# Maxima of attention one to two units ahead of the weights, and the selecting matrix loaded at the head of the second half

## The chip, the cores and the metric

The kernel runs on one core of a Trainium2 chip. The metric is device time in microseconds: the median over runs of one launch, lower is better. The engines are PE (matrix products), DVE (elementwise and reductions), ACT (activations), POOL (elementwise, selects, and issuing of some DMAs) and SP (issuing of DMAs). Each has its own instruction order and waits for the others by semaphores. A wait blocks everything that stands behind it on the same engine.

## The reference

The output is `g * a + (1 - g) * b` for 2048 positions of 448 channels, with a gate `g` of each position. `a` is a state space model applied as a long convolution, `b` is an attention in four segments with a memory that is carried from segment to segment:

```python
x = A_u                                              # 1 x 2048 x 448
g = sigmoid((x * gate_w).sum(-1, keepdims=True))
# a: kernel of 2048 taps for each channel, from 256 complex modes
P = exp((A * dt[:, None])[:, :, None] * pos)
K = 2.0 * einsum("dn,dnl->dl", C, P).real
a = irfft(rfft(u_t, 2 * L) * rfft(K, 2 * L))[:, :, :L]  (+ u * D_skip)
# b: 16 heads of 28, four segments s of 512 positions
logits = einsum("bhqd,bhkd->bhqk", qs, ks) * scale + mask      # causal in the segment
a_dot = einsum("bhqk,bhkd->bhqd", softmax(logits), vs)
a_mem = einsum("bhld,bhde->bhle", phi(qs), M) / (phi(qs) . z + 1e-6)
o = sigmoid(beta) * a_mem + (1 - sigmoid(beta)) * a_dot
M, z = M + phi(ks)^T vs, z + sum(phi(ks))
b = o @ wo
```

## The kernel before, in words

**First half** (to about 455 us): the modes' powers and the kernel K, and the projections to q, k and v, which are written to memory in a high and a low part each. Its order is written out, and the change leaves it alone.

**Second half** (`second_half`, L1256). It begins with `attend` (constants and the functions of attention), the loads of unit 0, `transform_k` (K's first step, eight steps long, 456 to 488 us) and `convolve` (the generator `cv`: spectra of the input, products with K's, and back). Then comes a loop over 16 **units** i of attention, each one segment and four heads (a "head group"), and in each unit six **rounds** r. Everything is written as generators; `step(x)` runs one of them up to its next yield. The order in which steps are called is PE's order; the other engines' orders follow nearly the same, with a scheduler free to move what isn't pinned.

What a unit consists of:

- `maxima(i)`, L1028: six steps. Each multiplies the high part of q with that of k for one block of the 512 x 512 logits and one pair of heads (PE, `ps_a<-ku,qu`), and DVE takes the maximum of each row (L1048, with the mask `mk` added). A seventh step does nothing. The eighth turns the maxima over (four transposes on PE, L1433, to `ps_m`), negates and splits them in a high part (ACT, L1058) and a low part (DVE, L1059), and POOL issues two DMAs (`qu<-mn`, L1061) that write them to row 28 of each head in the two parts of q.
- `weigh(i)`, L1064: six steps. Since k has ones in row 28, the products of q and k (PE, `ps_a<-qu,ku`, three products of parts for each tile, six matmuls or twelve) come out with the maximum subtracted. ACT takes exp (`PT`, L1081). After the sixth, POOL zeroes the upper triangles (L1086). The first matmul of each step reads row 28 of the high part, the fifth that of the low part.
- `values(i)`, L1088: at the second step, round 1 of the following unit, PT times V (`ps_pv<-PT,V`) and a copy.
- For segments, `seg_end`: normalising, recalling the memory and the product with `wo`; for the last segment `divide` and `last_end`.

Beside the units run, in the same loop: `rest` (projections of the input's spectra, units 1 to 8, rounds 1, 3, 4, 5; its results are multiplied with the spectra in `pr`, L611), `cv` (1.15 steps in each round of units 1 to 12), the last rows of the convolution in units 14 and 15, and `turn_over(n)`: n **dummy** matmuls of a constant (`ps_pv<-wz`), whose results nobody reads.

`ps_a` has three buffers, shared by maxima, weights and `rest`; `ps_m` and `ps_pv` have one each. So a step of PE waits until the step three before it has been read, by DVE (maxima) or ACT (exp).

Where the maxima stand: unit 0's are stepped among K's first step; two steps of unit 1's too, and four more between that and the loop, with three dummies each:

```python
for r in range(4):
    turn_over(3)
    step(ms[1])
```

In the loop, each round of unit i steps the maxima of unit i + 2 (`ahead`), and the seventh and eighth step of unit i + 1's (`behind`) come in rounds 0 and 1. `load(i + 3)` and `load_rest(i + 2)` at the head of each unit fetch q and k on SP's queue.

`load_wo`, L984, called at the end of unit 1, fills constants: `wo`, `den`, the row `dbc`, and `sel`, the **selecting matrix**. For that one, SP loads `selin` (L992) and ACT copies it to `sel` with rounding (L993). It is used first when the first segment is recalled.

Of the kernel before, what the change touches and what calls it, by code (L numbers as in the profile page):

```python
# [12 lines left out]
F32 = mybir.dt.float32  # L13
# [14 lines left out]
SEG = 512  # L28
# [948 lines left out]
def attend(nc, k, ap):  # L977
# [2 lines left out]
    wo = ap.tile([128, 4, D], F32, name="wo")  # L980
    k.den = ap.tile([128, 128], F32, name="den")
    k.sel = ap.tile([32, 4, 128], F32R, name="sel")

    def load_wo():  # L984
        nc.gpsimd.memset(wo, 0.0)
        for j in range(4):
            k.ldma(
                wo[32 * j : 32 * j + 28], k.wo.rearrange("(g j e) c -> j e g c", j=4, e=28)[j]
            )
        k.ldma(k.den, k.c_den)  # L990
        t = ap.tile([128, 4, SEG], F32, tag="am", name="selin", bufs=1)[:32, 0]
        k.ldma(t, k.c_sel.rearrange("p g c -> p (g c)"))  # L992
        nc.scalar.activation(k.sel.rearrange("p g c -> p (g c)"), t, AF.Copy)  # L993
        k.ldma(k.dbc, k.D_skip.unsqueeze(0).broadcast_to([128, D]))

    Q, K, W, Vs, pvss = {}, {}, {}, {}, {}
# [130 lines left out]
    am = {}  # L1127
# [128 lines left out]
def second_half(nc, k, ap, tp, fp, fin, lp):  # L1256

    none = object()  # L1260

    def step(g):
        return next(g, none) is not none

    nothing = iter(())
    attend(nc, k, ap)
    k.load(0)
    k.load_rest(0)


    wz = ap.tile([128, SEG], BF16, name="wz")
    nc.gpsimd.memset(wz, 1.0)

    def turn_over(n):
        pt = k.ps("pv")
        for _ in range(n):
            k.mm(pt, wz[:, :128], wz, start=True, stop=True)

    first = transform_k(nc, k, tp)
    ms = {i: k.maxima(i) for i in range(16)}  # L1280
    for r in range(8):
        step(first)
        if r == 1:
            k.load(1)
            k.load_rest(1)
        for _ in range((0, 1, 2, 1, 2, 1, 1, 0)[r]):
            step(ms[0])
        if r >= 6:
            step(ms[1])

    pm = k.ps("m")
    k.tr(pm[:16, :128], k.gt, k.ident)
    g16 = ap.tile([16, 128], F32, name="g16")
    nc.vector.tensor_copy(g16, pm[:16, :128])
    k.dma(k.GD.rearrange("(i p) -> i p", p=128), g16)
    k.gt2 = ap.tile([128, 16], F32, name="gt2")
    for h in range(2):
        k.dma(k.gt2[64 * h : 64 * h + 64], k.GD.rearrange("(n h w) -> h n w", h=2, w=16)[h])
    fp = fp()
    cv = convolve(nc, k, fp)  # L1300
    step(cv)
    k.load(2)
    vals = k.values(0)
    step(vals)
    for r in range(4):
        turn_over(3)
        step(ms[1])
    rest = project_rest(nc, k, lp())
    ends = []
    acc = 0.0  # L1310
    n = 0
    for i in range(16):
        k.load_rest(i + 2)
        k.load(i + 3)
        ahead = ms.get(i + 2, nothing)
        behind = ms.get(i + 1, nothing)
        w = k.weigh(i)
        for r in range(6):
            if 1 <= i < 9:
                if r in (1, 3, 4, 5):  # L1320
                    step(rest)
            elif r in WARM:
                turn_over(WARM[r])
            if i == 9 and r == 1:
                step(rest)
            step(ahead)
            step(w)
            if r == 0:
                step(behind)
            if r == 1:  # L1330
                if i > 0:
                    step(vals)
                step(behind)
                if i % 4 == 0 and i > 0:
                    ends.append(k.seg_end(i // 4 - 1))
            if r != 1 or i == 13:
                for _ in range(2 if i == 13 else 1):
                    while ends and not step(ends[0]):
                        ends.pop(0)
            if (i, r) in DIVIDE:  # L1340
                k.divide(DIVIDE[i, r])
            if 1 <= i <= 12:
                acc += RATIO
                while acc >= 1.0:
                    acc -= 1.0
                    step(cv)
            if i == 11 and r == 2:
                k.skip_last()
            if i == 13 and r < 5:
                load_b(r)  # L1350
            if i == 14 and r >= 2 or i == 15 and r < 4:
                last(n)
                turn_over(1)
                if n < 2:
                    join(n + 6)
                if n < 3:
                    load_b(n + 5)
                n += 1
        step(w)
        if i == 1:  # L1360
            k.load_wo()
        if i > 0:
            vals = k.values(i)
            step(vals)
        if i == 12:
            for _ in cv:
                pass
            load_b, join, last = finish(nc, k, fin())
        if i == 13:
            for wc in range(6):  # L1370
                join(wc)
    for e in ends:
        for _ in e:
            pass
    k.last_end(step, vals)
# [1 line left out]

RATIO = 1.15
WARM = {3: 1, 4: 3, 5: 3}
DIVIDE = {(14, 2): 0, (14, 5): 1, (15, 3): 2}  # L1380

# [286 lines left out]
```

## Time and profile before

| | us |
|---|---|
| median of 3 runs | 900.52 |
| lowest and highest | 894.51, 901.75 |
| the profiled execution | 905.99 |
| its span | 904.2 |
| PE busy | 767.8 (85%) |
| DVE busy | 600.0 (66%) |
| ACT busy | 537.1 (59%) |
| POOL busy | 191.0 (21%) |

The profile comes from one execution, which took 905.99 us; the span is from its first to its last recorded instruction. Rows of a timeline begin with the start in the span and the busy time of the group, then engine, line, operation, result and operands, and the number of instructions; in brackets the idle time ahead of it and what ended it. PEclk is the share of TensorE's full clock that was granted, in 40 slices of the span in tenths (9 is 90% and more), or in a window as a fraction. "DMA to landing" is the time from the issue of a DMA to its last byte.

### The profile page before, as it was taken

To read this page: it belongs to the slowest core of one execution; us is meant where nothing else is said; L and a number is where in the kernel's file an instruction comes from. 1 tells how busy PE (TensorE), PEld (TensorE's weight loads), DVE (VectorE), ACT (ScalarE), POOL (GpSimd) and SP (SyncE) were. 2 spreads that over 40 slices of the span, in tenths; PEclk is the share of its full clock that TensorE was granted. 3 is DMA by queue.
4 is the path that set the end of the run, shared out by engine and by line. 5 is a ranking of instruction groups with operands and counts; after the bars stand their busy time and mean duration, and the time that the engine had idled before them with its cause. 6 is when DMAs were issued, how large, how long until landed. Compare 5 with 4: busy or idle time off the path is not lost.

```text
span 904.2 us, 19002 instructions
## 1 busy us (share of the span) xinstructions
PE 767.8 (85%) x7508; PEld 413.7 (46%) x7517; DVE 600.0 (66%) x1158; ACT 537.1 (59%) x640; POOL 191.0 (21%) x273
## 2 busy tenths in 40 slices
PE   1676997899887999879787997999998999888997
PEld 1353654564454565446443443444444444334433
DVE  7985569766479757687857454556465656665564
ACT  4875689888789788888812344545354534342320
POOL 5222211011110011100100211232323232333210
PEclk9996999999898999989968597999999999888799
DMA  9258844223434324220377765678577575456773
GB/s 234 82 143 287 251 142 133 80 79 107 120 123 127 101 97 150 94 83 14 140 248 270 248 178 149 227 234 279 171 232 253 174 236 179 150 192 226 203 237 100
DMA packets 93408, 153.15 MB, mean 169 GB/s; under 512 B 21544, under 2 KB 58040, under 8 KB 93320
## 3 DMA queue, kind: packets, MB, share of 16 engines
q1 hardware_dynamic: 82104, 136.13, 47.6%
q10 hardware_dynamic: 8032, 10.26, 3.2%
q0 software_dynamic: 3184, 5.56, 2.3%
q8 instruction: 59, 0.97, 0.5%
q14 instruction: 29, 0.24, 0.1%
HBM read 90.91 MB, written 60.63 MB: 168 GB/s over the span
## 4 chain that ended last, share of the span: by engine, by line
PE 56%; DVE 16%; ACT 12%; DMA 8%; issue 5%; SPq 1%; POOL 1%; DVEq 0%; ACTq 0%; POOLq 0%
PE ps_m L1430 18%; PE ps_a L1430 18%; PE ps_pv L1430 8%; PE ps_arg L1430 6%; ACT cs L1395 5%; PE ps_k L1430 4%; DVE jk L1048 4%; DVE Y L402 3%; PE ps_m L1433 2%; DVE X L398 2%; DVE Y L403 1%; DMA RD<-rs 1%; DVE pr L611 1%; ACT hi L1395 1%; ACT L1395 1%
## 5 line engine op out<-in xcount | busy, mean ns | idle before, releaser
L1048 DVE CUSTOM_DVE_ANT_0 jk<-ps_a,mk 128x512 f32<-128x512 f32 (+3 forms) x256 | 125.0, 488 | 55.3 <-PE ps_a L1430 48.2
L1081 ACT ACTIVATE PT<-ps_a 128x1024 f32<-128x1024 f32 (+1 forms) x96 | 84.6, 882 | 119.4 <-PE ps_a L1430 110.1
L364 POOL TENSOR_TENSOR EX<-EX,cab 128x1024 f32<-128x1024 f32 x28 | 54.0, 1931 | 318.3 <-ACT EX L1395 274.2
L1395 ACT ACTIVATE cs<-ps_arg 128x1024 f32<-128x1024 f32 x111 | 107.3, 1020 | 9.7 <-PE ps_arg L1430 8.5
L1430 PE MATMUL ps_a<-qu,ku 32*128 32x512 f32 (+3 forms) x768 | 93.7, 366 | 8.5 <-ACT PT L1081 6.8
L1430 PE MATMUL ps_k<-Y,X 128*32 128x64 f32 x3584 | 67.2, 231 | 30.6 <-DVE Y L403 30.2
L1086 POOL TENSOR_SCALAR_AFFINE_SELECT PT<-PT 128x256 f32<-128x256 f32 x128 | 52.2, 421 | 182.6 <-ACT PT L1081 173.6
L398 DVE TENSOR_TENSOR X<-EX,cs 128x1024 f32<-128x1024 f32 x56 | 69.7, 1245 | 23.2 <-ACT cs L1395 23.1
L1430 PEld LDWEIGHTS ps_k<-Y,X 128*32 128x32 f32 x3584 | 57.5, 117 | 54.5 <-DVE Y L403 44.7
L1430 PE MATMUL ps_m<-xh,w 112*128 112x512 f32 x192 | 76.2, 440 | 1.7 <-ACT gs L1395 1.0
L1430 PEld LDWEIGHTS ps_a<-qu,ku 32*128 32x128 f32 x768 | 65.5, 203 | 16.9 <-ACT PT L1081 7.3
L402 DVE TENSOR_TENSOR Y<-EY,cs 128x1024 f32<-128x1024 f32 x56 | 70.0, 1250 | 0.0
L1430 PE MATMUL ps_arg<-ce,lh 64*128 64x512 bf16 x168 | 40.8, 443 | 30.6 <-ACT EY L1395 20.0
L1395 ACT ACTIVATE cs<-cs,bhp 128x1024 f32<-128x1024 f32 x56 | 64.4, 1151 | 1.8
L1430 PEld LDWEIGHTS <-lh 64*128 64x128 bf16 x392 | 22.5, 96 | 81.3 <-issue 69.1
L1395 ACT ACTIVATE EY<-ps_arg 128x1024 f32<-128x1024 f32 x52 | 52.1, 1040 | 9.2 <-PE ps_arg L1430 9.1
L1430 PE MATMUL ps_a<-ku,qu 32*128 32x512 f32 (+3 forms) x256 | 48.0, 415 | 9.8 <-DVE mx L1048 8.6
L1430 PEld LDWEIGHTS ps_a<-ku,qu 32*128 32x128 f32 x256 | 23.4, 199 | 57.6 <-issue 26.6
L1430 PEld LDWEIGHTS ps_m<-xh,w 112*128 112x128 f32 x192 | 38.1, 198 | 23.6 <-issue 9.4
L404 DVE SCALAR_TENSOR_TENSOR Y<-EY,cs 128x512 f32<-128x512 f32 x56 | 40.5, 725 | 11.7 <-ACT cs L1395 11.0
L1430 PE MATMUL ps_arg<-ct,lh 64*128 64x512 bf16 x224 | 45.3, 390 | 0.8 <-ACT cs L1395 0.8
L1430 PE MATMUL ps_pv<-PT,V 128*32 128x128 f32 (+3 forms) x512 | 45.0, 499 | 0.0
(229 smaller groups left out, 1462.0 us busy)
## 6 DMA issues: line engine op xcount, KB each, us to landing
w<-WD SPq DMA_DIRECT2D x24, 448.0 KB, 3.9
qu<-QD SPq DMA_DIRECT2D x32, 256.0 KB, 4.2
ku<-KD SPq DMA_DIRECT2D x32, 256.0 KB, 4.4
GU<-gs SPq DMA_DIRECT2D x32, 224.0 KB, 2.6
GK<-gs SPq DMA_DIRECT2D x8, 896.0 KB, 3.7
gk<-GK SPq DMA_DIRECT2D x32, 224.0 KB, 5.4
gu<-GU SPq DMA_DIRECT2D x32, 224.0 KB, 2.5
BB<-bs ACTq DMA_DIRECT2D x16, 448.0 KB, 4.8
```

The lines of the kernel that those rows point to most:

```text
L364: nc.gpsimd.tensor_tensor(o, o, cab, ALU.mult)
L398: v.tensor_tensor(X, ex, t[:, :, 0], ALU.mult)
L402: v.tensor_tensor(Y[:, :, :, :32], lo, y[:, :, :, ::-1], ALU.mult)
L403: v.tensor_tensor(Y[:, 0, :, 32:], ey[:, :, 32:], y[:, 0], ALU.mult)
L404: v.scalar_tensor_tensor(Y[:, 1, :, 32:], ey[:, :, 32:], -1.0, y[:, 1], ALU.mult, ALU.mult)
L611: nc.vector.tensor_tensor(pr[c], pt, ks.pop(c), ALU.mult)
L1048: v.tensor_tensor_reduce(junk[:, :n], pt[:, x, o : o + n], k.mk[:, SEG - n :], 1.0, -3e38, ALU.add, ALU.max, mx[:, 3 - t, h : h + 1],)
L1081: nc.scalar.activation(PT[b, hp], pt[:, :, :n], AF.Exp, scale=SCALE)
L1086: nc.gpsimd.affine_select(sl, sl, [[0, 2], [1, 128]], ALU.is_ge, 0.0, base=0, channel_multiplier=-1)
L1395: x = op(*args, **kw)
L1430: tc.keep_in_program_order(nc.tensor.matmul(*args, **kw))
L1433: tc.keep_in_program_order(nc.tensor.transpose(*args))
```

## The change

Two things change, both in the second half.

The selecting matrix is loaded at the head of the second half, on POOL's queue (`pdma`) and not SP's (`ldma`), and ACT's copy is called there.

The maxima run one to two units ahead. The four rounds ahead of the loop are gone. In unit i, rounds 0 to 3 step the maxima of unit i + 1 (its third to sixth step), rounds 4 and 5 step those of unit i + 2 (its first and second). The turning over of unit i + 1's maxima and the writing of row 28 come behind the weights of round 4 of unit i, where they came in rounds 0 and 1. Unit 0 has three dummies in every round, where it had one in round 3 and three in rounds 4 and 5. A step of a segment's end is left out in round 4 and not in round 1, and the divisions of the last segment move with that.

```diff
@@ attend
     k.sel = ap.tile([32, 4, 128], F32R, name="sel")
+    selin = ap.tile([128, 4, SEG], F32, tag="am", name="selin", bufs=1)[:32, 0]
+    k.pdma(selin, k.c_sel.rearrange("p g c -> p (g c)"))
+    nc.scalar.activation(k.sel.rearrange("p g c -> p (g c)"), selin, AF.Copy)
 
     def load_wo():
...
         k.ldma(k.den, k.c_den)
-        t = ap.tile([128, 4, SEG], F32, tag="am", name="selin", bufs=1)[:32, 0]
-        k.ldma(t, k.c_sel.rearrange("p g c -> p (g c)"))
-        nc.scalar.activation(k.sel.rearrange("p g c -> p (g c)"), t, AF.Copy)
         k.ldma(k.dbc, k.D_skip.unsqueeze(0).broadcast_to([128, D]))
@@ second_half
     step(vals)
-    for r in range(4):
-        turn_over(3)
-        step(ms[1])
     rest = project_rest(nc, k, lp())
...
             if 1 <= i < 9:
                 if r in (1, 3, 4, 5):
                     step(rest)
-            elif r in WARM:
-                turn_over(WARM[r])
+            elif i == 0 or r in WARM:
+                turn_over(3 if i == 0 else WARM[r])
             if i == 9 and r == 1:
                 step(rest)
-            step(ahead)
+            step(behind if r < 4 else ahead)
             step(w)
-            if r == 0:
+            if r == 4:
+                step(behind)
                 step(behind)
             if r == 1:
                 if i > 0:
                     step(vals)
-                step(behind)
                 if i % 4 == 0 and i > 0:
                     ends.append(k.seg_end(i // 4 - 1))
-            if r != 1 or i == 13:
+            if r != 4 or i == 13:
                 for _ in range(2 if i == 13 else 1):
                     while ends and not step(ends[0]):
                         ends.pop(0)
...
-DIVIDE = {(14, 2): 0, (14, 5): 1, (15, 3): 2}
+DIVIDE = {(14, 4): 0, (15, 0): 1, (15, 3): 2}
```

## The prediction

> **What bounds the kernel now.** I read the page first (busy time, slices, groups), then PE's waits from 455 us to the end, then the timelines of the stretches that the change touches, then windows of them.
>
> ```profile
> span 904.2 us, 19002 instructions
> PE 767.8 (85%) x7508; PEld 413.7 (46%) x7517; DVE 600.0 (66%) x1158; ACT 537.1 (59%) x640; POOL 191.0 (21%) x273
> PEclk9996999999898999989968597999999999888799
> ...
> L1048 DVE CUSTOM_DVE_ANT_0 jk<-ps_a,mk 128x512 f32<-128x512 f32 (+3 forms) x256 | 125.0, 488 | 55.3 <-PE ps_a L1430 48.2
> ```
>
> PE is busy for 85% of the span and the next engine for 66%; so time is won or lost where PE idles, or where its granted clock falls (the digits 6, 8, 5, 9, 7 in the middle of the PEclk line, near 500 and 550 us, are the lowest of the second half). The last row is the price of the work that is moved: 256 reductions of 488 ns on DVE, 16 in each unit. PE's waits in the second half, grouped (total, number, mean):
>
> ```profile
> PE ps_a L1430 <- DVE mx L1048: 11.3, 12, 3.0
> PE ps_a L1430 <- DVE pr L611: 7.0, 8, 3.3
> PE ps_a L1430 <- ACT PT L1081: 6.8, 1, 6.8
> ```
>
> The third is one wait of 6.8 us, for an exp; the first holds the one at the start of unit 0. Both are in the change's reach. Everything else in the second half is PE at work, and so what the change adds between units lands on the path.
>
> **Step 1: the start.** Removed ahead of unit 0 are four rounds of three dummies and a maxima step; unit 0 takes dummies in each round instead.
>
> ```profile
> 485.31 1.30 POOL L1061 DMA_DIRECT2D qu<-mn  x2 [28.88 <-ACT mn L1058]
> DMA to landing us min/median/max: 3.5/3.8/4.0
> 490.40 1.18 SPq L1446 DMA_DIRECT2D ku<-KD  x1
> 490.03 0.82 PE L1430 MATMUL ps_pv<-wz 128*128 128x512 bf16 x3
> 495.19 0.49 PE L1430 MATMUL ps_a<-ku,qu 32*128 32x512 f32 x2 [2.96 <-DVE mx L1048]
> 495.31 0.95 PE L1430 MATMUL ps_a<-qu,ku 32*128 32x512 f32 x6
> 510.03 1.65 PE L1430 MATMUL ps_a<-qu,ku 32*128 32x512 f32 x6
> 495.00:500.00 5.00, 4.21 (x24) 2.33 (x28) 3.27 (x12) 2.13 (x3) 0.42 (x2) 0.62 1.03 374
> 500.00:505.00 5.00, 4.47 (x33) 3.82 (x35) 4.05 (x17) 1.61 (x3) 2.28 (x5) 0.50 0.95 310
> 515.00:520.00 5.00, 5.00 (x37) 1.72 (x36) 0.67 (x2) 1.47 (x2) 0.41 (x1) 0.50 0.11 38
> ```
>
> (The landing row is that of mn's DMAs around 485 us. In windows the columns are length, PE, PEld, DVE, ACT and POOL busy with their counts, granted clock, DMA share and GB/s.) Unit 0's weights start at 495.31 and unit 1's at 510.03. The 2.96 us ahead of 495.19 are put down to mx, but unit 2's maxima step needs K's load issued at 490.40 as well, while the DMA engines are full. This idle brought the clock down to 0.50 until 520.
>
> In the changed kernel unit 0's weights hang on the two writes of row 28, issued at 485.31 and about 485.96: with 3.5 us to landing they can start at 489.4. A round is three dummies (0.82), a maxima step (about 0.4 at the full clock) and the weights (0.9): 2.1 us. Round 4 of unit 0 ends at 489.4 + 0.9 + 4 x 2.1 = 498.7. There the maxima of unit 1 are turned over; by the rows of step 3 the first write is issued 1.5 us later, at 500.2, and takes some 4 us in this full stretch: unit 1 starts at 504.2 and not at 510.03. Gain 5.8, taken as **6**. PE waits about 3 us at the end of unit 0 in this sum; it is in it. Bounds: 8 with a landing in 1.8 us; 1 if that wait brings the clock to 0.50 again and it stays there for 20 us from 504 on, 10 us more of half speed in unit 1 than before, 5 us.
>
> **Step 2: the selecting matrix.** Its load leaves SP's queue and its copy leaves ACT's order behind unit 1.
>
> ```profile
> 540.00 0.33 SPq L1446 DMA_DIRECT2D selin<-in_c_sel  x1
> 542.22 0.41 ACTq L625 DMA_DIRECT2D BB<-bs  x1
> 546.74 0.63 ACT L993 ACTIVATE sel<-selin 32x512 fp32r<-32x512 f32 x1 [9.34 <-DMA selin<-in_c_sel]
> 548.33 1.86 PE L1430 MATMUL ps_a<-qu,ku 32*128 32x384 f32 x12 [6.80 <-ACT PT L1081]
> 571.71 1.08 PE L1430 MATMUL ps_a<-qu,ku 32*128 32x384 f32 x12 [0.26 <-DVE pr L611]
> 549.00:556.00 7.00, 7.00 (x38) 4.04 (x34) 3.82 (x11) 2.65 (x4) 1.88 (x4) 0.62 0.37 119
> 445.00:456.00 11.00, 6.19 (x200) 4.28 (x197) 8.41 (x10) 4.64 (x6) 1.68 (x2) 0.81 0.15 46
> 459.39 0.92 ACT L567 ACTIVATE gs<-ps_a 128x896 f32<-128x896 f32 x1 [9.19 <-PE ps_a L1430]
> ```
>
> ACT stands at the copy until selin lands, the exps stand behind it, and PE waits 6.80 us for a buffer that an exp must empty. Until 542.22 ACT is held by its own issue of BB, which stays (its load is waited for). So the late part is 546.74 + 0.63 - 542.63 = 4.7 us. With them goes most of the idle time behind which the clock falls: twelve matmuls took 1.86 us, and 1.08 later; 7 us at 0.62 are 7 x 0.38 = 2.7 us. Gain 4.7 + 2.7 = 7.4, taken as **7**; bounds 4.7 (the 2.1 us left still bring the clock down) and 6.8 + 2.7 = 9.5 (BB's issue comes earlier too). The new place: the copy of 0.63 us falls before 459.39, in ACT's idle stretch of 9.19 us; the load goes on POOL's queue when DMA is busy for 0.15 of the time. Nothing waits there; if that cover were gone, 0.63.
>
> **Step 3: the turn between units.** Before, row 28 of a unit was written in rounds 0 and 1 of the unit ahead of it, some four rounds early. Now transposes, mn and the writes come behind round 4's weights, and the next unit's first matmul waits for them. How long that chain is, and what PE has meanwhile:
>
> ```profile
> 568.73 0.60 PE L1433 MATMUL ps_m<-ident,mx 128*4 128x128 f32 x4
> 569.36 0.59 ACT L1058 ACTIVATE mn<-ps_m 4x512 fp32r<-4x512 f32 x1
> 570.24 0.56 POOL L1061 DMA_DIRECT2D qu<-mn  x1 [2.19 <-ACT mn L1058]
> 570.96 0.56 POOL L1061 DMA_DIRECT2D qu<-mn  x1 [0.16 <-issue]
> DMA to landing us min/median/max: 1.8/3.5/5.8
> 580.12 0.73 PE L1430 MATMUL ps_pv<-xh,w 112*128 112x512 f32 x2
> 569.25 1.02 PE L1430 MATMUL ps_a<-gu,cf 64*128 64x448 f32 x4
> 541.03 0.50 PE L1430 MATMUL ps_a<-ku,qu 32*128 32x384 f32 x4
> 581.24 0.62 PE L1430 MATMUL ps_a<-qu,ku 32*128 32x256 f32 x6
> 582.97 0.96 PE L1430 MATMUL ps_a<-qu,ku 32*128 32x512 f32 x6
> ```
>
> (The landing row is over all of mn's DMAs.) From the transposes' start the high part is issued after 570.24 - 568.73 = 1.51 us and the low part after 2.23; with a landing L they are there at 1.51 + L and 2.23 + L. PE's work up to the next unit's first weights is transposes 0.60, a step of the convolution 0.73, the projections of round 5 1.02 (three dummies instead, 0.82), a maxima step 0.50, the weights of round 5 0.62, the convolution 0.73: 4.2, taken as 4.3 with part of the maxima step that opens the unit. The low part is needed four matmuls of six later, 0.64. With L = 3.5 the high part is late by 0.7, the low part by 0.8. Of fifteen turns, unit 0's is in step 1; six have more work between (wo's products, a spread, the last rows, the values of a new segment); eight remain: 8 x 0.8 = 6.4. At turns where DVE has the spectrum's products between the last two reductions it is up to 0.8 more, so I take **+7**. Bounds: nothing at L = 1.8 (PE is never out of work), 8 x 3.1 = 25 at 5.8. Behind the waiting matmul stand the convolution's matmuls and the values on PE, the unit's exps on ACT and the next reductions on DVE; all are in PE's order, so the wait isn't made up. On POOL the writes come behind one select and ahead of w's spreads, and hold up nothing that PE needs.
>
> A wait also costs clock:
>
> ```profile
> 585.46 1.86 PE L1430 MATMUL ps_a<-gk,cf 64*128 64x448 f32 x4 [1.52 <-DVE pr L611]
> 583.00:608.00 25.00, 23.05 (x152) 10.82 (x152) 14.52 (x44) 11.15 (x14) 8.55 (x18) 0.86 0.74 244
> ```
>
> Behind an idle stretch of 1.52 us four matmuls took 1.86 instead of 1.02, and 25 us ran at 0.86: 25 x 0.14 = 3.5 us for one drop. Waits of 0.8 are below the one seen; I take one turn that is longer: **+3** (bounds 0, and rival S). The Trainium skill, "TensorE: Matmul & The Clock Gate", section "The HAM clock gate (the 'warmup' mystery)", has the clock halve only after an idle window of about 3.4 us. By that rule these 3 us would be nothing; the row of 585.46, with a drop after 1.52 us, speaks against it.
>
> **Step 4: the end.** Four maxima steps that lay ahead of unit 0 now lie later, and unit 14 has maxima where it had none.
>
> ```profile
> 841.00:864.00 23.00, 22.41 (x135) 9.19 (x128) 12.46 (x20) 6.89 (x9) 4.73 (x11) 0.85 0.88 233
> ```
>
> Four steps are 4 x 16/6 x 0.488 = 5.2 us of DVE, which is busy for 12.46 of 23 there, and 4 x 0.50 = 2 us of PE, in part beside weights on other rows of the array: **+1**, bounds 0 and 5. The other order of segment ends and divisions moves the same work by a round or three: 0, bounds -3 and +3.
>
> **Sum:** -6 - 7 + 7 + 3 + 1 = **-2 us**. The profiled execution took 905.99 us (span 904.2), 5.5 above the median of the runs, 900.52; so 904.0 by the profile and 898.5 by the median.
>
> **Rivals.** *F, short landings.* If L at the turns is 2.8 or less, chain and work just meet: no wait, no drop, -6 - 7 + 1 = -12: 888.5. For it: the minimum is 1.8, and the DMA share is 0.37 from 549 to 556 and 0.74 from 583 to 608, where it is about 1 near 500. Against it: the median of 3.5 over all units. Beside it stands the Trainium skill, "DMA: Bandwidth & Descriptors", section "Anatomy of one DMA — SWDGE (gpsimd) path", which gives a small DMA about 2.0 us of fixed cost; by this estimate F would hold, but the median of this trace is well above. Chance 0.23.
>
> *S, each turn drops the clock.* From an idle time somewhere between 0.8 and 1.52 us on, a wait costs 3.5 of clock besides itself. With L of 4.2 and over at five turns (0.7 more each, 3.5) and five drops (17.5, one of which is in the sum with 3): -2 + 3.5 + 14.5 = +16: 916.5. For it: 12.46 of DVE work and w's spreads crowd the turns, and the median is near that point. Against it: at L = 3.5 the wait of 0.8 is half of the one that was seen to cost clock. This is the case that ends slower. Chance 0.20.
>
> *N, unit 0 gains nothing.* The clock falls at the end of unit 0 as it fell before it, step 1 brings 1 and not 6: -2 + 5 = +3: 903.5. For it: 3 us without work and full DMA engines. Against it: dummies in every round of unit 0. Chance 0.12.
>
> **How the numbers follow.** The forecast, 898.5, has 0.45: eight turns at 0.8 give or take 0.5, so 892 to 905. To leave out no more than 2 in 10 the range takes in F whole and the lower edge of S: 886 to 914. One per cent, 9 us, is about what a measurement of this kernel tells from no change. Faster by more (below 891.5): most of F and a little of the forecast, 0.24. Slower by more (over 909.5): S and the tail of N, 0.21. Within: 0.55.
>
> **What would show it.** Step 1: first weights of unit 0 near 489.4 and of unit 1 near 504, a PE wait of about 3 us between. Step 2: no 6.80 us ahead of an exp near 545, ACT going on right behind BB's issue. Step 3: waits of 0.5 to 1.2 us at eight turns, at the first or fifth matmul of a unit's weights, with the landing of qu<-mn as their end. Step 4: PE's busy share near 850 us as before. I am wrong if landings at the turns differ much from 3.5 us, or if the granted clock in units 1 to 12 moves by more than one drop.

## The result, and the profile after

| | before | after |
|---|---|---|
| median of 20 runs, us | 903.24 | 908.45 |
| lowest and highest | 894.51, 914.28 | 903.52, 920.41 |
| profiled execution, its span | 905.99, 904.2 | 905.38, 903.7 |

The ratio is 1.0103, with a 95% interval of 1.0076 to 1.0130: the changed kernel is about 1% slower, 5.2 us by the medians and 9 by the ratio. The ratios leave out the slow runs, those over 1.5% above the fastest of their kernel, and the medians do not; so the two can differ by some us. Two later measurements of the same kernel, beside the experiments, gave 1.0027 (0.9984 to 1.0071) and 1.0126 (1.0076 to 1.0177). The forecast was 898.5, slightly faster; the time lies in the range, but on the other side of the kernel before. The two profiled executions happen to be equally long, so they show where time moved, not the difference of the medians.

The page of after, the span and two of its lines; then PE's waits from 455 us to the end (total, number, longest):

```profile
span 903.7 us, 19007 instructions
PE 764.7 (85%) x7516; PEld 411.6 (46%) x7516; DVE 597.6 (66%) x1158; ACT 537.0 (59%) x640; POOL 192.1 (21%) x274
PEclk9996988999999989989987799899999997879799
```

```profile
PE ps_a L1427 <- DVE mx L1048: 24.3, 23, 8.4
PE ps_a L1427 <- DMA qu<-mn: 3.1, 2, 2.1
PE ps_a L1427 <- DVE pr L611: 2.4, 6, 0.6
```

The 6.8 us for an exp are gone and the waits for pr have shrunk from 7.0 to 2.4, but the waits for mx have grown from 11.3 us to 24.3, and one of them is 8.4 us long. The waits that I had forecast, for row 28 (`qu<-mn`), are 3.1 us in all.

Where does it stand? The table gives the length of each unit, from the start of its first weights to that of the next (unit 15: to the end of the span). It is read from the timelines of these executions: of before, of three of the changed kernel, and of two experiments. At its head stand K's first step (its first matmul to the turning over of unit 0's maxima) and the stretch from there to unit 0's first weights.

| | before | matrix alone (e1) | after | after (e4) | after (e16) | rows split (e9) |
|---|---|---|---|---|---|---|
| K's first step | 27.8 | 22.3 | 22.1 | 24.2 | 22.3 | 24.3 |
| to unit 0 | 11.5 | 11.8 | 6.1 | 6.1 | 6.2 | 6.1 |
| unit 0 | 14.7 | 14.7 | 18.2 | 14.5 | 21.7 | 14.1 |
| 1 | 21.9 | 20.2 | 22.3 | 22.3 | 22.7 | 22.8 |
| 2 | 31.1 | 23.0 | 22.6 | 21.8 | 22.0 | 22.5 |
| 3 to 10 | 197.1 | 196.0 | 199.9 | 205.3 | 202.0 | 206.0 |
| 11 | 24.1 | 23.5 | 31.1 | 30.6 | 30.2 | 21.4 |
| 12 and 13 | 56.4 | 57.2 | 58.1 | 58.5 | 58.3 | 58.3 |
| 14 and 15 | 63.6 | 63.4 | 67.0 | 66.6 | 67.0 | 67.4 |

In the three executions of the changed kernel, unit 0 starts 5.4 us sooner behind K's first step and unit 2 is 8 to 9 us shorter than in the kernel before; units 3 to 10 take 3 to 9 us more than in the two of the old order, 14 and 15 together 3 to 4, and unit 11 takes 6 to 8 us more, each time. The difference in units 3 to 10 is not so sure as it looks; the account of step 3 at the end comes back to it.

**The start**, in the timeline of after (PE and POOL):

```profile
478.26 0.60 PE L1430 MATMUL ps_m<-ident,mx 128*4 128x128 f32 x4
479.77 0.58 POOL L1061 DMA_DIRECT2D qu<-mn  x1 [23.23 <-DVE gs L569]
484.39 0.97 PE L1427 MATMUL ps_a<-qu,ku 32*128 32x512 f32 x6 [1.01 <-DMA qu<-mn]
502.60 2.08 PE L1427 MATMUL ps_a<-qu,ku 32*128 32x512 f32 x6 [2.85 <-DVE mx L1048]
```

As forecast, unit 0's weights follow the landing of row 28, and PE waits about 3 us (2.85) ahead of unit 1's.

**Unit 11.** In its round 2 the kernel fetches the last segment's four rows of the input (`skip_last`): SP loads a row, POOL multiplies it with `dbc` (L1172), DVE with the gate (L1187), and SP writes it to TB. There are three buffers for the rows. The timeline of after, in order of time:

```profile
757.79 3.46 POOL L1172 TENSOR_TENSOR xt<-xt,dbc 128x448 f32<-128x448 f32 x3 [6.81 <-DMA xt<-in_A_u]
758.95 3.05 DVE L1187 TENSOR_SCALAR xt<-xt,gt 128x448 f32<-128x448 f32 x3 [3.11 <-POOL xt L1172]
760.29 1.56 SPq L1443 DMA_DIRECT2D TB<-xt  x2
762.28 0.33 SPq L1443 DMA_DIRECT2D xt<-in_A_u  x1
765.25 1.13 POOL L1172 TENSOR_TENSOR xt<-xt,dbc 128x448 f32<-128x448 f32 x1 [3.49 <-DMA xt<-in_A_u]
766.41 0.57 DVE L1187 TENSOR_SCALAR xt<-xt,gt 128x448 f32<-128x448 f32 x1 [4.41 <-POOL xt L1172]
766.91 0.41 DVE L1048 CUSTOM_DVE_ANT_0 jk<-ps_a,mk 128x256 f32<-128x256 f32 x1
767.85 0.58 PE L1427 MATMUL ps_a<-ku,qu 32*128 32x256 f32 x2 [8.38 <-DVE mx L1048]
```

The fourth row has to wait until the first has been written out, then for its load, then for POOL. DVE stands for all of that, and behind its product stands the reduction that frees a buffer of `ps_a`: PE waits 8.38 us. In the kernel before, in the same unit, pr and reductions stood between the products:

```profile
770.63 3.25 DVE L1187 TENSOR_SCALAR xt<-xt,gt 128x448 f32<-128x448 f32 x2
773.80 1.07 DVE L611 TENSOR_TENSOR pr<-ps_a,ks 128x896 f32<-128x896 f32 x1
774.93 2.10 PE L1430 MATMUL ps_a<-pr,cb 128*64 128x448 f32 x8 [3.30 <-DVE pr L611]
775.27 0.44 DVE L1187 TENSOR_SCALAR xt<-xt,gt 128x448 f32<-128x448 f32 x1
779.27 0.57 DVE L1187 TENSOR_SCALAR xt<-xt,gt 128x448 f32<-128x448 f32 x1 [2.41 <-POOL xt L1172]
```

There the same rows cost PE the 3.30 us ahead of 774.93 (the longest wait for pr in the row of the prediction). The change has the maxima four rounds later, so that each round holds another of a unit's six steps than before; DVE's order came out with the four products in one piece. The 8.38 us aren't all that unit 11 pays: over it the granted clock was 0.75, against 0.86 in the kernel before.

### The profile page after: what moved, and what is told of

The parts are those of the page before. It is cut to its first block, busy times and chain, and to the rows that moved or that the text cites. A ratio compares the mean times of both kernels' runs of the same rounds, so it can differ in the third digit from the quotient of the medians.

```text
span 903.7 us, 19007 instructions
## 1 busy us (share of the span) xinstructions
PE 764.7 (85%) x7516; PEld 411.6 (46%) x7516; DVE 597.6 (66%) x1158; ACT 537.0 (59%) x640; POOL 192.1 (21%) x274
## 4 chain that ended last, share of the span: by engine, by line
PE 59%; DVE 14%; ACT 13%; DMA 7%; issue 5%; POOL 1%; SPq 1%; DVEq 0%; ACTq 0%; POOLq 0%
PE ps_m L1427 20%; PE ps_a L1427 19%; PE ps_pv L1427 9%; ACT cs L1392 6%; PE ps_arg L1427 5%; PE ps_k L1427 4%; DVE jk L1048 3%; DVE Y L402 2%; PE ps_m L1430 2%; DVE X L398 2%; DMA qu<-mn 1%; DVE Y L403 1%; DMA dn<-pvs 1%; DMA xt<-in_A_u 1%; ACT L1392 1%
## 5 line engine op out<-in xcount | busy, mean ns | idle before, releaser
L1086 POOL TENSOR_SCALAR_AFFINE_SELECT PT<-PT 128x256 f32<-128x256 f32 x128 | 53.1, 428 | 210.7 <-ACT PT L1081 208.9
L398 DVE TENSOR_TENSOR X<-EX,cs 128x1024 f32<-128x1024 f32 x56 | 69.7, 1245 | 22.2 <-ACT cs L1392 22.1
L1427 PEld LDWEIGHTS ps_a<-qu,ku 32*128 32x128 f32 x768 | 64.7, 200 | 23.9 <-DVE mx L1048 14.5
L1427 PE MATMUL ps_arg<-ce,lh 64*128 64x512 bf16 x168 | 40.5, 438 | 30.1 <-ACT EY L1392 18.9
L1427 PE MATMUL ps_a<-ku,qu 32*128 32x512 f32 (+3 forms) x256 | 47.7, 407 | 14.6 <-DVE mx L1048 13.5
L1427 PEld LDWEIGHTS <-lh 64*128 64x128 bf16 x392 | 22.3, 95 | 80.5 <-issue 68.4
L1427 PEld LDWEIGHTS ps_a<-ku,qu 32*128 32x128 f32 x256 | 23.8, 200 | 65.1 <-issue 22.4
L611 DVE TENSOR_TENSOR pr<-ps_a,ks 128x896 f32<-128x896 f32 x32 | 34.7, 1085 | 20.5 <-PE ps_a L1427 18.6
```

The source lines that it names most:

```text
L398: v.tensor_tensor(X, ex, t[:, :, 0], ALU.mult)
L611: nc.vector.tensor_tensor(pr[c], pt, ks.pop(c), ALU.mult)
L1086: nc.gpsimd.affine_select(sl, sl, [[0, 2], [1, 128]], ALU.is_ge, 0.0, base=0, channel_multiplier=-1)
L1427: tc.keep_in_program_order(nc.tensor.matmul(*args, **kw))
```

## The experiments

"C", "D" and so on are theories, named where they first appear. "The time" of an experiment is its median with the ratio to the kernel before, timed on the same chip; two experiments can come from different chips, so they are compared by these ratios.

**e1: the selecting matrix alone**, in the kernel before.

```diff
     k.sel = ap.tile([32, 4, 128], F32R, name="sel")
+    selin = ap.tile([128, 4, SEG], F32, tag="am", name="selin", bufs=1)[:32, 0]
+    k.pdma(selin, k.c_sel.rearrange("p g c -> p (g c)"))
+    nc.scalar.activation(k.sel.rearrange("p g c -> p (g c)"), selin, AF.Copy)
...
-        t = ap.tile([128, 4, SEG], F32, tag="am", name="selin", bufs=1)[:32, 0]
-        k.ldma(t, k.c_sel.rearrange("p g c -> p (g c)"))
-        nc.scalar.activation(k.sel.rearrange("p g c -> p (g c)"), t, AF.Copy)
```

> The kernel before with only the selecting matrix's load and copy moved to the head of the second half. Theory A (the new place pays as step 2 says, and the reordering is what loses): 6 to 9 us below the kernel before, so about 895 us, and no PE wait of 6.8 us for an exp near 545 us. Theory B (the gain of the start of unit 2 is made up by later waits): within 2 us of the kernel before.

Measured: 898.33, ratio 0.9938 (0.9891 to 0.9985), so 5.6 us faster by the ratio. The copy moved into ACT's idle time:

```profile
449.61 0.54 POOL L984 DMA_DIRECT2D selin<-in_c_sel  x1 [9.46 <-DVE Y L403]
454.14 0.61 ACT L985 ACTIVATE sel<-selin 32x512 fp32r<-32x512 f32 x1
```

**e2: the reordering alone**, the changed kernel with the three lines put back in `load_wo`.

> The changed kernel with the selecting matrix loaded and copied where it was, so the reordering alone. Theory A: 6 to 9 us above the changed kernel, so about 916 us, 1.4% above the kernel before. Theory B: within 2 us of the changed kernel.

Measured: 912.12, ratio 1.0128 (1.0078 to 1.0178). Against the three measurements of the changed kernel (1.0027 to 1.0126, mean 1.0085) the matrix is worth about 4 us there, a difference within the intervals; in the profile unit 2 took 29.3 us, after 22.6 in the changed kernel. At its old place the matrix costs PE a shorter wait than in the kernel before (2.91 us and not 6.80), since ACT comes to it later beside its load:

```profile
538.26 0.63 ACT L993 ACTIVATE sel<-selin 32x512 fp32r<-32x512 f32 x1 [2.83 <-DMA selin<-in_c_sel]
540.22 1.87 PE L1427 MATMUL ps_a<-gu,cf 64*128 64x448 f32 x4 [2.91 <-ACT ks L606]
```

So theory A holds in its signs: the matrix gains, the reordering by itself loses.

**e3: the fourth row six rounds later**, in round 2 of unit 12 (the expectation says nine).

```diff
-    def skip_last():
+    def skip_last(rows):
...
-        for t in range(4):
+        for t in rows:
...
             if i == 11 and r == 2:
-                k.skip_last()
+                k.skip_last(range(3))
+            if (i, r) == (12, 2):
+                k.skip_last([3])
```

> The changed kernel, with the fourth of the last segment's rows of the input (skip_last) fetched and multiplied nine rounds later, in round 2 of unit 12, so that no reduction of the maxima stands on DVE behind the product that waits for its reload. Theory C (the wait of 8.4 us in unit 11, behind that fourth row, is where the reordering loses): the wait falls below 2 us, unit 11 takes 25 us and not 31, and the time falls by 5 to 8 us, to about 902. Theory D (the loss is spread over the turns between units, where the weights wait for row 28): the time stays within 2 us of 908.

Measured: 908.6, ratio 1.0063 (1.0019 to 1.0107). Unit 11 fell to 23.8 us, as theory C has it, but units 12 and 13 rose to 24.1 and 42.0. The row now collides there with the end of the third segment, which uses the same buffers, in two waits of PE:

```profile
794.79 1.01 PE L1429 MATMUL ps_a<-qu,ku 32*128 32x256 f32 x6 [4.89 <-DVE mx L1048]
829.52 0.68 PE L1429 MATMUL ps_m<-r,sel 32*128 32x512 f32 x1 [4.29 <-ACT tb L1178]
```

The edit moved the stall rather than removing it, so the time, level with the changed kernel's, decides nothing between C and D.

**e4 and e16: the changed kernel again.**

> The changed kernel as it is, for a second profile and time beside the others on the same chip. Theory C: the wait of about 8 us in unit 11 is there again, within 1 us. Theory D: it was that execution's, and another unit has one. Time about 908.

> The changed kernel as it is, a third time: 1.003 to 1.010 of the kernel before, with the wait of 8 to 8.6 us in unit 11.

Measured: 906.93, ratio 1.0027 (0.9984 to 1.0071), and 911.49, ratio 1.0126 (1.0076 to 1.0177). The wait in unit 11 was 8.5 and 8.1 us: it belongs to the kernel and not to one execution. The last ratio lies a little above what was expected.

**e5: a buffer of its own for the fourth row.**

```diff
-        xt = ap.tile([128, D], F32, tag="xt", name="xt", bufs=3)
+        own = i == 15
+        xt = ap.tile([128, D], F32, tag="tb" if own else "xt", name="xt", bufs=2 if own else 3)
```

> The changed kernel, with the fourth of the last segment's rows of the input in a free buffer of its own (one of tb's), where it is, so that its load needn't wait for the first row's way out. Theory C (the fourth row's way through memory holds up DVE, and PE behind it, in unit 11): the wait of 8.4 to 8.5 us falls to about 4 (POOL's four products of 1.13 stay ahead), nothing later grows, and the time falls by 4 to 5 us from the changed kernel's 907 to 908.5. Theory G (what is gained there is lost again in units 12 and 13, as with the row put off): unit 12 takes 24 us and not 21, and the time stays.

Measured: 903.47, ratio 1.0037 (0.9999 to 1.0074). PE's waits for `ps_a` from 745 to 790 us:

```profile
PE ps_a L1428 <- DVE mx L1048: 5.5, 2, 4.7
PE ps_a L1428 <- DMA qu<-mn: 1.8, 2, 1.5
```

The long wait went from 8.4 to 4.7, near what C has. Unit 11 took 28.6 us (after: 31.1), and units 12 and 13 took 59.6 (after: 58.1), so of 2.5 us gained in unit 11 the profile keeps 1. The median is 3 to 5 us below the first two of the changed kernel, but the ratio is not below that of e4, 1.0027, on the same chip. This run doesn't decide between C and G.

**e9: the rows' products spread over four rounds.** The buffer of e5, and each product on DVE behind the reductions of a round of its own (`k.reduced` is the last reduction called); the loads stay where they are.

```diff
+        rows = [skip(3, t) for t in range(4)]
+        yield
         for t in range(4):
-            xt = skip(3, t)
+            xt = rows[t]
             i = 12 + t
-            v.tensor_scalar(xt, xt, k.gt[:, i : i + 1], None, ALU.mult)
+            with k.issue_after(k.reduced.ins):
+                v.tensor_scalar(xt, xt, k.gt[:, i : i + 1], None, ALU.mult)
             k.dma(k.TB[128 * i : 128 * i + 128], xt)
+            yield
...
-            if i == 11 and r == 2:
-                k.skip_last()
+            if (i, r) == (11, 2):
+                rows = k.skip_last()
+            if (11, 2) <= (i, r) <= (12, 0):
+                step(rows)
```

> The changed kernel, with the loads of the last segment's four rows where they are and the fourth in its own buffer, and their four products on DVE one in each of the next rounds, behind that round's reductions. Theory C: no wait over 1 us in unit 11, which takes 23 to 25 us and not 31, with nothing added after: 6 to 8 us below the changed kernel, 900 to 902. Theory G (the loss moves to units 12 and 13): within 2 us of the kernel with the fourth row's own buffer, 903.5.

Measured: 901.52, ratio 0.9984 (0.9943 to 1.0025). In its timeline DVE reduces while POOL is still at the rows, and PE's waits for `ps_a` from 745 to 790 us are short:

```profile
758.00 4.44 POOL L1173 TENSOR_TENSOR xt<-xt,dbc 128x448 f32<-128x448 f32 x4 [5.61 <-DMA xt<-in_A_u]
758.82 0.42 DVE L1048 CUSTOM_DVE_ANT_0 jk<-ps_a,mk 128x256 f32<-128x256 f32 x1 [2.47 <-PE ps_a L1434]
762.43 0.62 DVE L1191 TENSOR_SCALAR xt<-xt,gt 128x448 f32<-128x448 f32 x1
```

```profile
PE ps_a L1434 <- DMA qu<-mn: 2.0, 2, 1.2
PE ps_a L1434 <- DVE mx L1048: 1.6, 2, 0.8
```

Unit 11 takes 21.4 us and not 30 to 31, at a granted clock of 0.92, and units 12 and 13 together take 58.3, as in the changed kernel. With this one stall gone, the changed kernel is level with the kernel before. Theory C is shown, as the largest single loss; G falls.

**e12: the same in the kernel before**, with the matrix of e1 as well.

> The kernel before with the selecting matrix moved and the rows' products one in each round. The kernel with the matrix alone has one wait of 3.3 us for pr behind these rows: it goes, and the time falls by 2 to 4 us from that kernel's 898, to 894 to 896, below every kernel so far. If what is gained there is given back in unit 13, 898.

Measured: 893.4, ratio 0.9913 (0.9875 to 0.9951): faster than both kernels, and the best that was run. The rows are worth 0.25% to e1, 2.3 us, which the intervals don't tell from nothing, against about 1% to the changed kernel. The profiles say the same: units 11 to 13 took 78.1 us here and 80.7 in e1, but 79.7 in e9 and 89.2 in the changed kernel. Between e12 and e9 lies the reordering with the stall taken out: 0.9984 - 0.9913 = 0.7%, 6 us **slower**, its gain at the start included. Between e1 and the changed kernel it is 1.0085 - 0.9938 = 1.5%. So the stall is about half of what the reordering loses; where the other half lies is not shown as clearly.

**e7 and e8: the early start with the order of before.** The four rounds ahead of the loop are removed; unit 0 steps unit 1's last four maxima steps beside unit 2's six. Unit 0 keeps the three dummies of every round, and the matrix stands where the change has it. e8 adds e5's buffer.

```diff
-    for r in range(4):
-        turn_over(3)
-        step(ms[1])
...
+            if i == 0 and r < 4:
+                step(behind)
             step(ahead)
             step(w)
+            if i == 0 and r == 4:
+                step(behind)
+                step(behind)
```

> The kernel before with the selecting matrix moved and unit 0 at once behind K's first step: unit 0 steps both unit 1's last four maxima steps and unit 2's six, from unit 1 on the order is that of the kernel before. Theory E (the early start is a gain, and the later order of the changed kernel is the loss): unit 0 starts near 484 to 488, unit 1 near 503, units 2 to 15 take what they take with the selecting matrix alone, and the time is 5 to 8 us below the 898.3 of that kernel, about 892. Theory B (a start that is earlier by 6 to 11 us is given back somewhere after, whatever the order): within 2 us of 898.

> The kernel of the early start with the order of before, and the fourth row in a buffer of its own. Theory C: the wait of some 3 us for pr behind the rows in unit 11 gets shorter, 1 to 3 us below the kernel with the early start, about 890. Theory G: within 1 us of it.

Measured: 898.22, ratio 0.9978 (0.9945 to 1.0010), and 900.39, ratio 1.0022 (0.9984 to 1.0060). Neither says what was asked of the start: unit 0 started no sooner behind K's first step (12.2 and 12.0 us), since its first round steps unit 2's maxima, and so waits for that unit's loads (6.97 us of PE in e7, put down to `ku<-KD`); and unit 0 took 18.9 us with two maxima steps in a round, at a granted clock of 0.50 and 0.53. Of e8's own question they do say something: with the old order the buffer brought nothing (unit 11 took 24.9 us, after 24.1 in e7), where theory C had 1 to 3 us. An early start with the old distance of two units is not to be had this way.

**e6: the turning over one round earlier**, behind round 3.

```diff
     step(vals)
+    step(ms[1])
     rest = project_rest(nc, k, lp())
...
-            step(behind if r < 4 else ahead)
+            step(behind if r < 3 else ahead)
...
-            if r == 4:
+            if r == 3:
                 step(behind)
                 step(behind)
...
-            if r != 4 or i == 13:
+            if r != 3 or i == 13:
```

> The changed kernel with the maxima one round further ahead: transposes and the writing of row 28 behind round 3 and not round 4 of the unit before, with one step more of unit 1 ahead of the loop. Theory D (the units' first weights wait for row 28): the waits on qu<-mn, 2.1 to 2.4 us at unit 13 and 1.3 at unit 11, go, each of units 1 to 12 gets 0.8 us shorter, and the time falls by 6 to 9 us. Theory H (the landing is mostly hidden; the loss at the turns is DVE's order, reductions behind the projections' lo and e): only the waits named for qu<-mn go, 3 us in all, and the units' first weights still wait for mx. Unit 11 may change by itself, since the rows of the input fall otherwise on DVE.

Measured: 919.45, ratio 1.0209 (1.0164 to 1.0255). The waits for row 28 did go (0.5 us left from 455 to 545, none named later), yet the time rose by 11 us, which neither theory had. The page's line of PE shows 15 us more of busy time than in after:

```profile
PE 779.9 (85%) x7507; PEld 423.9 (46%) x7516; DVE 592.7 (65%) x1158; ACT 537.3 (59%) x640; POOL 189.8 (21%) x274
```

My edit had moved the maxima by one round, an odd number, and so each step onto the pair of heads that the weights of its round use. Then a step's weights start 0.34 us behind its maxima:

```profile
561.42 0.50 PE L1428 MATMUL ps_a<-ku,qu 32*128 32x512 f32 x2
561.76 0.96 PE L1428 MATMUL ps_a<-qu,ku 32*128 32x384 f32 x12
```

**e10: the pairs exchanged**, in e6.

```diff
-    MSTEPS = [(b, 1 - hp) for b, hp in STEPS]
+    MSTEPS = STEPS
```

> The kernel with the turning over behind round 3, with the pairs of heads of the maxima exchanged as well, so that a maxima step again uses the two row groups of the array that the weights of its round leave free. Theory I (the 11 to 18 us that the earlier turning over cost came from maxima and weights on the same row groups, one behind the other): PE's busy time goes back from 780 to about 766 us, and the time falls from 919 to 900 to 905. Theory D adds: below the changed kernel by 5 or more, for the waits on qu<-mn and the drops of clock behind them. Theory J (the row groups make no difference; the earlier turning over stalls DVE or ACT): above 912 still, with PE busy for 775 or more.

Measured: 915.34, ratio 1.0190 (1.0146 to 1.0233). The same step, now 0.01 us apart, the page's line of PE, and PE's waits from 455 us on:

```profile
560.90 0.50 PE L1428 MATMUL ps_a<-ku,qu 32*128 32x512 f32 x2
560.91 1.07 PE L1428 MATMUL ps_a<-qu,ku 32*128 32x384 f32 x12
```

```profile
PE 769.1 (84%) x7507; PEld 413.1 (45%) x7516; DVE 592.7 (65%) x1158; ACT 536.8 (59%) x640; POOL 190.3 (21%) x274
```

```profile
PE ps_a L1428 <- DVE mx L1048: 19.3, 18, 4.0
PE ps_m L1428 <- DVE mn L1059: 5.6, 2, 3.7
```

PE's busy time falls by 11 us, so theory I is right on the row groups; but the time falls by 4 alone by the medians and 1.7 by the ratios, which the intervals don't tell from nothing. In place of the overlap there are waits: in units 3 to 10 PE's waits sum to 16.0 us (10.7 in e6, 12.4 in the changed kernel), and these units take 211.5 (210.7 and 199.9), at a granted clock of 0.94 (0.95 and 0.98). Unit 13 takes 43.7 us here and 43.6 in e6, after 37.4 in the changed kernel, with one wait of 3.7 us (3.8 in e6) for mn in `ps_m`, which has one buffer and which the segment's end uses as well. So there is a stall as J has it, besides what I says. Row 28 a round earlier buys nothing.

**e11: both**, e10 with the rows of e9.

> Both of the two: maxima one round further ahead with the pairs exchanged, and the rows' products one in each round. If the two losses (unit 11's stall, the turns) are separate, the gains add up: 892 to 898, below the kernel before. If one hides the other: 898 to 903.

Measured: 912.14, ratio 1.0064 (1.0021 to 1.0108): the rows help here as well, by 1.3% by the ratios (the medians say 0.3%), but the sum stays above the kernel before and above e9, and neither expectation holds.

**e13: the turning over one round later**, in e9.

```diff
-            if r == 4:
+            if r == 5:
                 step(behind)
                 step(behind)
```

> The kernel with the rows' products one in each round (from the changed kernel), with transposes and the writing of row 28 one round later still, behind round 5. Theory D (at round 4 the writes already land later than the weights need them): each turn gets longer by the whole of the work of a round that lies between, 1.5 to 2 us, 20 to 26 us in fourteen turns, more with drops of the clock: 922 to 935. Theory H (at round 4 the landing is mostly hidden): part of the round's work was slack, less than 1 us for each turn: 905 to 915.

Measured: 981.77, ratio 1.0909 (1.0842 to 1.0976): 80 us from e9, 5.7 for each of fourteen turns, far more than either theory. The landings of mn's DMAs and what PE waited for over the whole span, and one turn:

```profile
DMA to landing us min/median/max: 1.8/5.2/6.8
  PE ps_a L1434: 53.6, 19
```

```profile
560.09 0.60 PE L1437 MATMUL ps_m<-ident,mx 128*4 128x128 f32 x4
562.92 0.56 POOL L1061 DMA_DIRECT2D qu<-mn  x1 [0.75 <-DVE mn L1059]
567.35 1.22 PE L1434 MATMUL ps_a<-qu,ku 32*128 32x512 f32 x4 [4.57 <-DMA qu<-mn]
```

A round of slack is lost, the landing gets longer by 2.1 us in the median (3.1 in e9), and the clock falls. The last is seen in windows from 545 to 750 us, of the matrix alone, of after and of e13, in this order (length, PE, PEld, DVE, ACT and POOL busy, clock, DMA share, GB/s):

```profile
545.00:750.00 205.00, 191.55 (x1288) 91.70 (x1290) 125.90 (x360) 97.77 (x124) 59.28 (x114) 0.99 0.68 219
```

```profile
545.00:750.00 205.00, 192.47 (x1265) 91.89 (x1266) 123.35 (x352) 94.77 (x121) 57.97 (x112) 0.97 0.68 218
```

```profile
545.00:750.00 205.00, 171.28 (x1030) 80.33 (x1029) 92.53 (x270) 77.39 (x98) 44.45 (x90) 0.84 0.55 172
```

PE is busy for 171 us and not 192, and what it does runs at 0.84. At round 4, where the change has the writes, most of the landing is still covered, and one round later it is not.

**e14: the divisions as before**, in e9.

```diff
-DIVIDE = {(14, 4): 0, (15, 0): 1, (15, 3): 2}
+DIVIDE = {(14, 2): 0, (14, 5): 1, (15, 3): 2}
```

> The same kernel with the divisions of the last segment in rounds 2 and 5 of unit 14, as before the change. If their new places cost the 2.5 us that unit 14 got longer: unit 14 takes 23.7 and not 26, and the time falls by 2 to 3 us from 901.5. If the maxima that now lie in unit 14 cost it (theory K): unit 14 stays at 25 to 26.6 us and the time within 1 us.

Measured: 905.04, ratio 0.9993 (0.9945 to 1.0040), against e9's 0.9984: no difference. Units 14 and 15 take 67.9 us (e9: 67.4; before: 63.6). So the places of the divisions cost nothing. That leaves theory K, that the maxima now in unit 14 cost it, but K was not tried directly, and two other profiles speak against its size: e5 and e15 have the same maxima and divisions there, and their unit 14 took 23.9 and 24.0 us, units 14 and 15 together 64.7 and 64.8. PE's waits in unit 14 are 2.6 us in these two and in the changed kernel alike (0.4 in the kernel before). What differs is the granted clock in that unit: 0.86 and 0.85, and 0.78 in the changed kernel. So over half of the 3 to 4 us is clock, and why it fell in some executions alone is open.

**e15: three dummies ahead of the first weights** of units 1 to 12, in e9.

```diff
             step(behind if r < 4 else ahead)
+            if r == 0 and 1 <= i <= 12:
+                turn_over(3)
```

> The same kernel with three more dummies ahead of the first weights of units 1 to 12, 0.82 us in each at the full clock. If the clock that falls behind the waits at the turns is the larger cost: the granted clock from 500 to 750 us rises to 0.98 or more, and the time falls by 2 to 4 us. If the waits are there in most units but cost only themselves: no change, since the dummies fill them. If most turns have no wait: 12 x 0.8 = 10 us slower.

Measured: 902.44, ratio 1.0053 (1.0014 to 1.0092). By the medians 9.8 us of dummies cost 1, by the ratios 6: between "the waits are there and are filled" and "most turns have no wait". The granted clock from 500 to 750 us was 0.95, after 0.94 in e9 and not the 0.98 of the first expectation. The dummies gain nothing and don't buy the clock back; how much of the loss is wait and how much clock stays open.

## Why the prediction was wrong, by its own steps

**What was missed: the rows of the input in unit 11.** The sum has no term for it. The step that failed is the reading ahead of step 1, "everything else in the second half is PE at work", with step 4's "the other order of segment ends and divisions moves the same work by a round or three: 0". I followed what the shift of the maxima does on PE, ACT and POOL, and on DVE at the turns and in unit 14, but not what it does to every other instruction that shares DVE's order with the reductions. The row was in my own fence: waits for pr with 7.0 us in 8. Its third number, 3.3, is the longest wait and not the mean, as I had it; it is the 3.30 us in unit 11, and I didn't ask what stood ahead of it on DVE. In its place PE waits 8.4 us for mx, and unit 11 is longer by 7; e9, which takes the stall away, brings 1.0% by the ratios (1.0085 - 0.9984), of which the old order would have gained 0.25% as well. Adding 7 us to the forecast's -2 gives +5, and the medians differ by 5.2. That they meet is partly luck, since the other terms were off in both directions, as follows.

**Step 1, the start.** Unit 0's weights 5.4 us sooner behind K's first step, a wait of 2.85 ahead of unit 1: both as forecast (5.9 and 3). But from K's first matmul to unit 1's first weights, five executions of the changed order (after, e2, e4, e9, e16) took 46.5, 47.7, 44.8, 44.5 and 50.1, and three of the old (before, e1, e12) 54.0, 48.8 and 48.6: the gain is 2 to 4 us by means (46.7 against e1, and against all three), less than 6. Where K's first step took 27.8 at a granted clock of 0.64 (e2), unit 0 took 14.2 at 0.98; where it took 22.1 and 22.3 at 0.93 and 0.90 (after, e16), unit 0 took 18.2 and 21.7 at 0.56 and 0.58. So in these a stretch at half clock falls in one or the other, and rival N was half right: part of what is gained in order is lost to the clock.

**Step 2, the matrix.** 7 forecast; 5.6 by e1 and about 4 by e2 in time, 8 and 7 in unit 2 of their profiles. Right in kind, and inside the bounds but for the time of e2.

**Step 3, the turns.** 7 + 3 forecast, and this step failed too. PE's waits in units 3 to 10, where most of the eight turns lie, sum to 12.4, 13.7 and 11.9 us in the three executions of the changed kernel, and to 11.3 and 12.6 in before and e1: the new waits at the turns took the place of others (those for pr fell from 7.0 to 2.4), and the 7 us aren't there as a sum. These units were still longer, by 4 to 9 us against e1, at a granted clock of 0.98, 0.95 and 0.96 against 0.99. But e12, e7 and e8, with the old order there, took 199.0, 202.5 and 202.6 at 0.97, 0.96 and 0.96. So this length goes with the clock of an execution, and that the reordering lowers that clock is not shown. Units 12 and 13 took about 1 us more than in e1. The landings were shorter than the 3.5 us that I took:

```profile
DMA to landing us min/median/max: 2.0/3.0/6.3
```

and PE's waits named for them were 3.1, 10.9 and 9.3 us in three executions of the changed kernel, of which 1.0, 5.0 and 5.8 belong to the first two units. More often a unit's first weights wait for DVE (eight units in after, six in e4, seven in e16), where the projections' lo and e come between the last reductions. After, the start of unit 4:

```profile
566.45 0.69 DVE L966 TENSOR_TENSOR lo<-ps_pv,hi 128x512 fp32r<-128x512 f32 x1
567.06 0.60 DVE L967 TENSOR_SCALAR e<-e 128x512 f32<-128x512 f32 x1
567.58 0.68 DVE L1048 CUSTOM_DVE_ANT_0 jk<-ps_a,mk 128x512 f32<-128x512 f32 x1
568.32 0.96 PE L1427 MATMUL ps_a<-qu,ku 32*128 32x512 f32 x6 [0.86 <-DVE mx L1048]
```

I had this as an extra of the term, and it is the commoner wait of the two. e6 and e10 show that waits for row 28 could be had away, at a higher price elsewhere.

The 3 us of clock rested on one wait of 1.52 us in the kernel before, behind which four matmuls took 1.86 us. e1 has the same wait ahead of the same matmuls, and there it cost nothing: they took 1.02 us, and the 25 us around them ran at a granted clock of 1.00.

```profile
574.19 1.02 PE L1430 MATMUL ps_a<-gk,cf 64*128 64x448 f32 x4 [1.52 <-DVE pr L611]
```

So the length of a wait alone didn't decide, and "3.5 us for one drop" was no price of a wait. The Trainium skill, "TensorE: Matmul & The Clock Gate", section "The HAM clock gate (the 'warmup' mystery)", has the clock halve only after an idle window of some 3.4 us. The stretch from 545 to 750 us speaks against it: in after and e9 it ran at 0.97 and 0.94, and PE had no wait of over 2.4 us in it.

**Step 4, the end.** +1 forecast, 3 to 4 in units 14 and 15 of the changed kernel, inside the bounds. With e5 and e15 (1.3 and 1.4 us above e1) the size is near the forecast, and the rest is the lower clock of unit 14; e14 shows that the divisions are not it.

**The rivals.** F had its condition half met (median 3.0 against 2.8) and its result not at all. What S describes, waits at the turns and a lower clock behind them, is seen in e13 (0.84), one round later than the change has it.

## What to carry to other kernels

When work is moved that shares an in-order engine with other work, list what stands beside it on that engine at the new place, all along the kernel and not only at the edited lines: here, four products, the last of which waits for a load, had been standing apart among other work of DVE, and came together ahead of a reduction that PE waits for. A work item that waits for memory belongs behind the work that frees PE's buffers (e9); a buffer of its own alone did not decide it (e5). The same edit gives the fastest kernel here with the old order (e12), though its gain over e1 is not clear of noise. And a distance between producer and reader should be tested on both sides: one round less cost 80 us, and one round more took the waits away but cost 7 to 11 us by what it met there.

## What the hardware showed unexpectedly

- Maxima and weights on different row groups of the array run beside each other (0.01 us between their starts in e10), on the same ones behind each other (0.34 us in e6): 769.1 and 779.9 us of PE busy time for the same matmuls.
- The landing of an 8 KB write isn't constant: a median of 3.0 us where it is issued in round 4, and 5.2 in round 5. In the turn of e13 shown above SP issues four loads of q and k between 560.77 and 562.26, around the two writes; that these loads are the cause was not tried.
- Behind a wait of 1.52 us the same four matmuls took 1.86 us in one execution (before) and 1.02 us in another (e1): what a wait costs in clock can't be read off its length alone.
- K's first step, which the change leaves alone, took between 22.1 and 27.8 us, at granted clocks of 0.93 and 0.64, a difference larger than most that were asked about here; single profiles are to be compared by stretches with a common beginning.
